# A Fourier convolution before two MoE layers: sums and differences over mirrored positions, one fp32 contraction in the second transform stage

## The chip, the cores and the metric

One core of a Trainium2 chip runs the whole program. The metric is the device time of one execution in microseconds; three runs of the kernel before took 2845.25, 2845.48 and 2846.35 us, median 2845.48. TensorE (PE) multiplies matrices into PSUM, VectorE (DVE) and ScalarE (ACT) read PSUM and SBUF, GpSimd (POOL) works on SBUF, SyncE (SP) issues DMAs.

## What is computed

A long convolution along the sequence, done by Fourier transforms, gated by its own input, and two feed-forward layers behind it:

```python
batch, seq, d_model = 2, 12480, 128
h_filt = (np.maximum(pos_emb @ w1, 0.0) @ w2) * np.exp(-0.01 * pos)[:, None]
u = x * v
y = irfft(rfft(u, 2 * S) * rfft(h_filt, 2 * S)[None], 2 * S)[:, :S]
x = (x * y).reshape(B * S, D)          # 24960 tokens of 128
h = x @ w_in;   x = (h * np.cos(h)) @ w_out            # d_ff 2048
h = x @ w_in2;  x = (h * clip(h + 3, 0, 6) / 6) @ w_out2
```

All inputs are fp32.

## The kernel before

The transform has length N = 111 x 113 (a prime-factor split, `N1` = 111 and `N2` = 113). The sequence sits in a grid of 111 partitions by 113 columns, and two transforms of this length, of the signal and of the signal times the alternating sign `sig`, take the place of one of double length. The 113 columns of a channel stand in mirrored order: 0 to 56, then the mirror of 1 to 56.

First comes the filter stage: 15 chunks of up to four columns for each half (`mlp`, `filt`). PE makes `rp` (plain fp32, one weight tile `w1b`) and then `hps` (`fp32r` matmuls in threes), ACT rounds `rh`, DVE takes the rest `rl`, and DVE multiplies `hps` by the window into three tiles of `h`. The pool `ps_r` holds two `rp` banks. The constants are issued as DMAs from ACT's queue at chunks 5 and 7, the input tiles from SP's.

Then the convolution loop, `NG` = 64 turns, each for two channels of both batches. Software pipelining is written out by hand, and `manual_schedule` keeps each engine's instructions in the order of the code. Turn i does, for PE:

- `s1(i+1, 2)`, `s1(i+1, 0)`, `s1(i+1, 1)`: the first forward stage for the filter and the two batches. Four plain fp32 matmuls each; the data (`h`, `hm`, `u`, 113 columns) is the loaded operand and the constant `f1` (112 columns) is streamed. ACT rounds the result `ap` to `fp32r` (`ah`), DVE subtracts for the rest (`al`).
- between them `s2i(i-2, 0)` and `s2i(i-2, 1)`: the first inverse stage, plain fp32, `bp`; again ACT rounds (`bh`) and DVE takes the rest (`bl`).
- `s2h(i)` and `s2u(i)`: the second forward stage, into `xh` and `xp`. Each of the two outputs (real, imaginary) takes two contractions over 113 rows, and each contraction three `fp32r` matmuls (`cs_h` x `ah`, `cs_h` x `al`, `cs_l` x `ah`): 12 matmuls for `xh` (224 columns) and 12 for `xp` (448).
- `s1i(i-2)`: the last inverse stage, two contractions of three `fp32r` matmuls, `v1` and `v2`.

An fp32 matmul shows as two records in the trace, an `fp32r` one as one. DVE multiplies the spectra (`mk_pq`: `pq` and, in place, `xp`), sums them (`mk_y`), and makes `w` out of `v1` and `v2s`, a copy by ACT (`mk_w`, with a small ACT copy of one column ahead of it). POOL makes `u` = x * v and its product with `sig` (`make_u`), `hm` = h * `sig` (`make_hm`), and the gated output `z` (`fin`), which SP stores. Beside this, `step_decode` unpacks the MoE weights in 16 pieces: four instructions each on DVE (those that fall together make three in one turn and one in another), four on ACT, two on POOL.

PSUM is full: two banks `ps_a` (for `ap` and `xh`), two `ps_x`, two `ps_b`, two `ps_v`. After the loop a tail finishes three channel pairs and hands the first tokens to the MoE stage, which fills the rest of the time.

Of the kernel before, what the change touches and what calls it, by code (L numbers as in the profile page):

```python
# [43 lines left out]
def kernel(  # L44
# [103 lines left out]
    def conv_phase(cctx):  # L148
# [14 lines left out]
        sig = const.tile([NP1, N2], FP32, name="sig")  # L163
        cs_h = const.tile([N2, 3, MP], F32R, name="cs_h")
        cs_l = const.tile([N2, 3, MP], F32R, name="cs_l")
        g_h = const.tile([2 * K1, 2, NP1], F32R, name="g_h")
        g_l = const.tile([2 * K1, 2, NP1], F32R, name="g_l")
# [679 lines left out]
```

## Time and profile before

| | us |
|---|---|
| median of 3 runs | 2845.48 |
| the profiled execution | 2846.66 |
| its span | 2844.9 |
| PE busy | 2812.9 |
| DVE busy | 2419.4 |
| POOL busy | 2406.7 |
| ACT busy | 2156.5 |

The span is what the profiler saw between the first and the last instruction; 1.8 us of the execution lie outside. Busy shares are means over three stages (filter, convolution, MoE) that differ, so the sections below read single stages. In the rows, a time is in microseconds from the start of the span; "x8" is a number of records put together; in square brackets stands how long the engine was idle and what ended that.

### The profile page before, as it was taken

The numbers are of one execution on the slowest core, as the hardware profiler recorded it, in microseconds if no ns is written. First come the engines' busy times: TensorE is split into PE (matmuls) and PEld (weight loads), VectorE is DVE, ScalarE is ACT, GpSimd is POOL, SyncE is SP. The second block draws the span as 40 slices with busy tenths as digits, with TensorE's granted clock in tenths as the row PEclk, the third lists the DMA queues.
The fourth block names the chain that finished last, engine by engine and source line by source line (L and its number), as shares of the span: only waits on it lengthen the run. The fifth ranks groups of instructions, "written<-read, shape, count | busy, mean of one in ns | idle before, by whom it ended". The sixth has DMA issues, their size and how long they took to land.

```text
span 2844.9 us, 41000 instructions
## 1 busy us (share of the span) xinstructions
PE 2812.9 (99%) x14089; PEld 2342.2 (82%) x14089; DVE 2419.4 (85%) x3271; ACT 2156.5 (76%) x3084; POOL 2406.7 (85%) x1390
## 2 busy tenths in 40 slices
PE   8999999998999999999999999999999999999999
PEld 6999999987888888888888888888888888888888
DVE  6888888887888888888888888888888888888887
ACT  2555545448888888888888888888888888888885
POOL 2788888767888888888888888888888889888887
PEclk9999999998999999999999999999999999999999
DMA  3233323210000000000000000000000000000000
GB/s 111 67 92 84 90 78 84 70 50 24 8 16 16 8 16 8 15 16 8 16 8 16 8 16 16 8 15 8 16 16 8 16 8 16 14 10 16 8 8 11
DMA packets 88273, 79.39 MB, mean 28 GB/s; under 512 B 57129, under 2 KB 78852, under 8 KB 88068
## 3 DMA queue, kind: packets, MB, share of 16 engines
q1 hardware_dynamic: 87182, 76.18, 9.7%
q8 instruction: 113, 1.85, 0.3%
q14 instruction: 92, 0.75, 0.1%
q10 hardware_dynamic: 886, 0.60, 0.1%
HBM read 51.00 MB, written 25.74 MB: 27 GB/s over the span
## 4 chain that ended last, share of the span: by engine, by line
PE 91%; DVE 3%; DMA 2%; POOL 1%; ACT 1%; issue 1%; SPq 0%; POOLq 0%; DVEq 0%; ACTq 0%
PE acc L680 38%; PE hb L614 19%; PE ha L614 19%; PE ap L229 4%; PE xp L340 4%; PE xh L340 3%; PE bp L395 2%; PE v L418 2%; DMA scr<-z 1%; DVE y L371 1%; DVE pq L361 1%; DVE xp L361 1%; POOL z L459 1%; POOL z L468 0%; PE hps L287 0%
## 5 line engine op out<-in xcount | busy, mean ns | idle before, releaser
L670 POOL TENSOR_TENSOR lo<-g,hi 128x1024 fp32r<-128x1024 f32 (+1 forms) x390 | 937.4, 2404 | 240.2 <-PE ha L614 162.4
L645 POOL TENSOR_TENSOR lo<-g,hi 128x1024 fp32r<-128x1024 f32 (+1 forms) x392 | 942.4, 2404 | 10.2 <-ACT hi L642 7.6
L635 DVE TENSOR_TENSOR g<-ha,r 128x512 f32<-128x512 f32 (+1 forms) x768 | 499.8, 691 | 289.1 <-ACT r L634 289.1
L624 ACT ACTIVATE k<-ha,biasq 128x512 int32<-128x512 f32 (+1 forms) x768 | 510.3, 689 | 310.2 <-PE ha L614 305.9
L614 PE MATMUL ha<-xh,wi 128*128 128x512 f32 (+1 forms) x1536 | 548.3, 398 | 10.8 <-ACT xh L591 7.7
L614 PE MATMUL hb<-x2h,vi 128*128 128x512 f32 (+1 forms) x1564 | 554.0, 395 | 0.3 <-DVE g L635 0.3
L634 ACT ACTIVATE r<-r,biaspi 128x512 f32<-128x512 f32 (+1 forms) x776 | 520.5, 721 | 0.2
L625 DVE SCALAR_TENSOR_TENSOR r<-k,ha 128x512 f32<-128x512 int32 (+1 forms) x768 | 490.0, 679 | 3.7 <-ACT k L624 3.2
L653 DVE SCALAR_TENSOR_TENSOR g<-q,hb 128x1024 f32<-128x1024 f32 (+1 forms) x391 | 473.2, 1210 | 9.0 <-ACT q L652 9.0
L667 DVE SCALAR_TENSOR_TENSOR hi<-q,hb 128x1024 fp32r<-128x1024 f32 (+1 forms) x390 | 470.1, 1205 | 0.0
L652 ACT ACTIVATE q<-hb,bias 128x1024 f32<-128x1024 f32 (+1 forms) x391 | 435.2, 1113 | 21.4 <-PE hb L614 18.3
L680 PE MATMUL acc<-hi,wo 128*128 128x512 f32 (+1 forms) x1568 | 430.7, 396 | 0.0
L680 PE MATMUL acc<-hi,vo 128*128 128x512 f32 (+1 forms) x1568 | 427.3, 394 | 0.0
L642 ACT CAST hi<-g 128x1024 fp32r<-128x1024 f32 (+1 forms) x388 | 403.6, 1040 | 0.0
L614 PEld LDWEIGHTS ha<-xh,wi 128*128 128x128 f32 x1536 | 289.3, 188 | 80.0 <-issue 11.9
L614 PEld LDWEIGHTS hb<-x2h,vi 128*128 128x128 f32 x1564 | 295.6, 189 | 70.3 <-ACT k L624 0.7
L680 PEld LDWEIGHTS acc<-hi,wo 128*128 128x128 f32 x1568 | 296.8, 189 | 68.4
L680 PEld LDWEIGHTS acc<-hi,vo 128*128 128x128 f32 x1568 | 294.5, 188 | 65.2
L614 PE MATMUL hb<-x2l,vi 128*128 128x512 f32 (+1 forms) x782 | 307.5, 393 | 0.0
L614 PE MATMUL ha<-xl,wi 128*128 128x512 f32 (+1 forms) x768 | 302.4, 394 | 0.0
L680 PE MATMUL acc<-lo,wo 128*128 128x512 f32 (+1 forms) x784 | 246.7, 396 | 0.0
L680 PE MATMUL acc<-lo,vo 128*128 128x512 f32 (+1 forms) x784 | 243.9, 392 | 0.0
(150 smaller groups left out, 3882.2 us busy)
## 6 DMA issues: line engine op xcount, KB each, us to landing
x<-in_x_dram SPq DMA_DIRECT2D x64, 197.8 KB
v<-in_v_dram SPq DMA_DIRECT2D x64, 197.8 KB
scr<-z SPq DMA_DIRECT2D x128, 98.9 KB
out_dram<-o SPq DMA_DIRECT2D x47, 256.0 KB
xf<-scr SPq DMA_DIRECT2D x17, 256.0 KB
wst<-in_wi_dram SPq DMA_DIRECT2D x8, 512.0 KB
wst<-in_wo_dram SPq DMA_DIRECT2D x8, 512.0 KB
pt<-in_post_dram SPq DMA_DIRECT2D x14, 224.0 KB
```

What stands on the lines that cost most here:

```text
L614: nc.tensor.matmul(out=hs[c][:, 0, :n], lhsT=w["i", e][:, sl], rhs=r[:, :n], start=(k == 0), stop=(k == 2))
L624: nc.scalar.activation(out=k[:, c, :n], in_=h, func=ACTF.Identity, bias=biasq, scale=1.0 / TWO_PI)
L625: nc.vector.scalar_tensor_tensor(out=un.r[:, c, :n], in0=k[:, c, :n], scalar=-TWO_PI, in1=h, op0=ALU.mult, op1=ALU.add)
L634: nc.scalar.activation(out=rc, in_=rc, func=ACTF.Sin, bias=biaspi, scale=1.0)
L635: nc.vector.tensor_tensor(out=un.g[:, c, :n], in0=h, in1=rc, op=ALU.mult)
L642: nc.scalar.copy(un.hi[:, :, :n], un.g[:, :, :n])
L645: nc.gpsimd.tensor_tensor(out=un.lo[:, :, :n], in0=un.g[:, :, :n], in1=un.hi[:, :, :n], op=ALU.subtract)
L652: nc.scalar.activation(out=un.r[:, c, :n], in_=h, func=ACTF.Relu, bias=bias3, scale=1.0)
L653: nc.vector.scalar_tensor_tensor(out=un.g[:, c, :n], in0=un.r[:, c, :n], scalar=6.0, in1=h, op0=ALU.min, op1=ALU.mult)
L667: nc.vector.scalar_tensor_tensor(out=un.hi[:, c, :n], in0=un.r[:, c, :n], scalar=6.0, in1=h, op0=ALU.min, op1=ALU.mult)
L670: nc.gpsimd.tensor_tensor(out=un.lo[:, :, :n], in0=un.g[:, :, :n], in1=un.hi[:, :, :n], op=ALU.subtract)
L680: nc.tensor.matmul(out=acc[e][:, :n], lhsT=w["o", e][:, sl], rhs=r[:, c, :n], start=(u == 0 and c == 0 and k == 0), stop=(u == KFF // 2 - ...
```

## The change

The first forward stage no longer carries the 113 columns but their sums and differences with the mirrored position. The column order becomes 1 to 56, 0, and then the mirror of 1 to 56, padded to `MP` = 114, so that both halves have 57. The sum of the halves stands in rows 0 to 56 of the first stage's result, the difference in rows 64 to 120 (`OD` = 64, `KE` = 121), and the rows between are zero. Cosines apply to sums, sines to differences, so real and imaginary part of the second stage are one contraction over 121 rows each, in plain fp32, and the splitting into `fp32r` parts falls away, in the inverse stages too.

```diff
+        def make_q(i):
+            if i >= NG:
+                return
+            q = q_t[i] = p_u.tile([N1, B, 2, CH, M2], FP32, tag="q", name="q")
+            nc.gpsimd.tensor_tensor(
+                out=q[:, :, 0], in0=x_t[i][:N1, :, :, M2:], in1=v_t[i][:N1, :, :, M2:], op=ALU.mult
+            )
+            for b in range(B):
+                nc.gpsimd.tensor_tensor(out=q[:, b, 1], in0=q[:, b, 0], in1=sg(1, CH), op=ALU.mult)
+
         def make_u(i):
             if i >= NG:
                 return
-            u = u_t[i] = p_u.tile([N1, B, 2, CH, N2], FP32, tag="u", name="u")
-            v = v_t.pop(i)
-            nc.gpsimd.tensor_tensor(out=u[:, :, 0], in0=x_t[i][:N1], in1=v[:N1], op=ALU.mult)
+            q, v, u = q_t.pop(i), v_t.pop(i), uf[i % 2]
+            p = ps_p.tile([N1, B, 2, CH, M2], FP32, tag="p", name="p")
+            nc.vector.tensor_tensor(
+                out=p[:, :, 0], in0=x_t[i][:N1, :, :, :M2], in1=v[:N1, :, :, :M2], op=ALU.mult
+            )
             for b in range(B):
-                nc.gpsimd.tensor_tensor(
-                    out=u[:, b, 1], in0=u[:, b, 0],
-                    in1=sig[:N1].unsqueeze(1).to_broadcast([N1, CH, N2]), op=ALU.mult,
-                )
-
-        def make_hm(i):
+                nc.vector.tensor_tensor(out=p[:, b, 1], in0=p[:, b, 0], in1=sg(0, CH), op=ALU.mult)
+            pf, qf, f = (t.rearrange("p b s c n -> p (b s c) n") for t in (p, q, u))
+            for o, op in ((0, ALU.add), (OD, ALU.subtract)):
+                nc.vector.tensor_tensor(out=f[:, :, o:o + M2], in0=pf, in1=qf, op=op)
...
+        def make_hf(i):
             if i >= NG:
                 return
-            hm = hm_t[i] = p_u.tile([N1, CH, N2], FP32, tag="hm", name="hm")
+            hm = p_u.tile([N1, CH, MP], FP32, tag="hm", name="hm")
+            h = h_of(i * CH, CH)
             nc.gpsimd.tensor_tensor(
-                out=hm, in0=h_of(i * CH, CH),
-                in1=sig[:N1].unsqueeze(1).to_broadcast([N1, CH, N2]), op=ALU.mult,
+                out=hm, in0=h, in1=sig[:N1].unsqueeze(1).to_broadcast([N1, CH, MP]), op=ALU.mult
             )
-
-        ps_a = cctx.enter_context(tc.tile_pool(name="ps_a", bufs=2, space=PSUM))
-
-        def s1(i, g):
+            for s_, t in enumerate((h, hm)):
+                for o, op in ((0, ALU.add), (OD, ALU.subtract)):
+                    nc.gpsimd.tensor_tensor(
+                        out=hf[i % 2][:, s_, :, o:o + M2], in0=t[:, :, :M2], in1=t[:, :, M2:], op=op
+                    )
+
+        def s1(i, g, pool=None):
             if i >= NG:
...
-            if True:
-                ap = ps_a.tile([N2, 4, 2 * K1], FP32, tag="a", name="ap")
-                for q in range(4):
-                    s, c = divmod(q, CH)
-                    if g < 2:
-                        st = u_t[i][:, g, s, c, :]
-                    elif s == 0:
-                        st = h_of(i * CH + c)[:, 0, :]
-                    else:
-                        st = hm_t[i][:, c, :]
-                    nc.tensor.matmul(out=ap[:, q, :], lhsT=st, rhs=f1)
-                nc.scalar.copy(ah[:, 4 * g:4 * g + 4, :], ap)
-                nc.vector.tensor_tensor(
-                    out=al[:, 4 * g:4 * g + 4, :], in0=ap, in1=ah[:, 4 * g:4 * g + 4, :], op=ALU.subtract
-                )
+                a_t[i] = p_2.tile([KE, 2, 12, K1], FP32, tag="at", name="at")
+            at = a_t[i]
+            ap = (pool or ps_a).tile([KE, 4, 2, K1], FP32, tag="a", name="ap")
+            for q in range(4):
+                s, c = divmod(q, CH)
+                st = (uf[i % 2][:, g, s, c] if g < 2 else hf[i % 2][:, s, c])[:, :KE]
+                nc.tensor.matmul(out=ap[:, q].rearrange("p z k -> p (z k)"), lhsT=st, rhs=f1)
+            src = ap.rearrange("p q z k -> p z q k")
+            nc.scalar.copy(at[:OD, :, 4 * g:4 * g + 4, :], src[:OD])
+            nc.scalar.copy(at[OD:, ::-1, 4 * g:4 * g + 4, :], src[OD:])
...
-            ps_r = hctx.enter_context(tc.tile_pool(name="ps_r", bufs=2, space=PSUM))
+            ps_r = hctx.enter_context(tc.tile_pool(name="ps_r", bufs=1, space=PSUM))
...
                 hps = ps_h.tile([N1, CB, 2, D], FP32, tag="hps", name="hps")
+                raw = hr.tile([N1, CB, 2, D - HS[2]], FP32, tag="raw", name="raw")
...
+                nc.scalar.copy(raw[:, :n], hps[:, :n, :, HS[2]:])
                 for e in range(2):
-                    m = min(n, (M2, N2 - M2)[e] - c0)
-                    if m <= 0:
-                        continue
+                    m = n
                     j0 = e * M2 + c0
-                    for q, t in enumerate(h_p):
+                    nc.gpsimd.tensor_tensor(
+                        out=h_p[2][:, :, j0:j0 + m].rearrange("p d c -> p c d"),
+                        in0=raw[:, :m, e],
+                        in1=win[:, j0:j0 + m].unsqueeze(2).to_broadcast([N1, m, D - HS[2]]),
+                        op=ALU.mult,
+                    )
+                    for q, t in enumerate(h_p[:2]):
...
                 filt(k)
+                if k == len(chunks) - 3:
+                    make_u(0)
                 if k >= len(chunks) - 2:
                     s1(0, k - len(chunks) + 2)
+                if k == 3:
+                    nc.sync.dma_start(out=sig, in_=c_sig)
+                    load(0)
+                    nc.sync.dma_start(out=f1, in_=c_f1)
+                    nc.sync.dma_start(out=cs, in_=c_cs)
                 if k == 5:
-                    nc.scalar.dma_start(out=sig, in_=c_sig)
-                    load(0)
-                    nc.scalar.dma_start(out=f1, in_=c_f1)
-                    nc.scalar.dma_start(out=cst, in_=c_cs)
-                    make_u(0)
+                    make_q(0)
+                    load(1)
+                    nc.sync.dma_start(out=f2, in_=c_f2)
+                    nc.sync.dma_start(out=gm, in_=c_g)
                 if k == 7:
-                    load(1)
-                    nc.scalar.dma_start(out=f2, in_=c_f2)
-                    nc.scalar.dma_start(out=gst, in_=c_g)
-                    make_u(1)
+                    make_q(1)
                 if k == 9:
                     load(2)
-                    for hi, lo, st in ((cs_h, cs_l, cst), (g_h, g_l, gst)):
-                        nc.scalar.copy(hi, st)
-                        nc.gpsimd.tensor_tensor(out=lo, in0=st, in1=hi, op=ALU.subtract)
...
-        ps_b = cctx.enter_context(tc.tile_pool(name="ps_b", bufs=1, space=PSUM))
+        ps_c = cctx.enter_context(tc.tile_pool(name="ps_c", bufs=1, space=PSUM))
         ps_v = cctx.enter_context(tc.tile_pool(name="ps_v", bufs=1, space=PSUM))
+
         def s2_mm(o, q0, q1, a):
-            ah, al = a
-            hr, hm_, lr, lm = (t[:, q0:q1, z * K1:(z + 1) * K1] for t in (ah, al) for z in range(2))
-            for z, terms in ((0, ((0, hr, lr), (1, hm_, lm))), (1, ((0, hm_, lm), (2, hr, lr)))):
-                k = 0
-                for m, h_, l_ in terms:
-                    for w_, r_ in ((cs_h, h_), (cs_h, l_), (cs_l, h_)):
-                        nc.tensor.matmul(out=o[z], lhsT=w_[:, m, :N2], rhs=r_, start=(k == 0), stop=(k == 5))
-                        k += 1
+            for z in range(2):
+                nc.tensor.matmul(out=o[z], lhsT=cs[:, z, :], rhs=a[:, z, q0:q1, :])
...
         def s2h(i):
-            ap = ps_a.tile([N2, 2, 4, K1], FP32, tag="a", name="xh")
+            ap = ps_c.tile([N2, 2, 4, K1], FP32, tag="a", name="xh")
             s2_mm((ap[:, 0], ap[:, 1]), 8, 12, a_t[i])
...
+        def s2i(i, g, pool=None):
+            if not 0 <= i < NG:
+                return
+            if i not in b_t:
+                b_t[i] = p_2.tile([2 * K1, 8, MP], FP32, tag="b", name="b")
+            src = (pool or ps_a).tile([2 * K1, 4, MP], FP32, tag="a", name="bp")
+            for q in range(4):
+                nc.tensor.matmul(out=src[:, q, :], lhsT=y_t[i][:, 4 * g + q, :], rhs=f2)
+            nc.scalar.copy(b_t[i][:, 4 * g:4 * g + 4, :], src)
...
-            for z, o, sl in ((1, v2, slice(MC, MP)), (0, v1, slice(0, MC))):
-                for k, (w_, r_) in enumerate(((g_h, bh), (g_h, bl), (g_l, bh))):
-                    nc.tensor.matmul(out=o, lhsT=w_[:, z, :], rhs=r_[:, :, sl], start=(k == 0), stop=(k == 2))
-            v1_t[i], v2_t[i] = v1, v2
...
+                    v = ps_v.tile([NP1, 2, 512], FP32, tag="v", name="v")
+                v2_t[i] = p_1.tile([NP1, 8, M2], FP32, tag="v2s", name="v2s", bufs=2)
+                v1_t[i] = [v[:, z, :8 * M2].rearrange("p (a b) -> p a b", b=M2) for z in range(2)]
+            v, b = v1_t[i], b_t[i]
+            r = slice(0, 8) if bs is None else slice(4 * bs, 4 * bs + 4)
+            for z in (1, 0):
+                nc.tensor.matmul(out=v[z][:, r], lhsT=gm[:, z, :], rhs=b[:, r, z * M2:(z + 1) * M2])
+            nc.scalar.copy(v2_t[i][:, r], v[1][:, r])
...
                 r = slice(0, 8) if isinstance(b, slice) else slice(4 * b, 4 * b + 4)
-                nc.scalar.copy(o[:, :, 0:1], v1[:, r, 0:1])
-                eng.tensor_tensor(out=o[:, :, 1:M2], in0=v1[:, r, 1:M2], in1=v2s[:, r], op=ALU.add)
-                eng.tensor_tensor(out=o[:, :, M2:], in0=v1[:, r, 1:M2], in1=v2s[:, r], op=ALU.subtract)
+                for h, op in ((0, ALU.add), (M2, ALU.subtract)):
+                    nc.vector.tensor_tensor(out=o[:, :, h:h + M2], in0=v1[:, r], in1=v2s[:, r], op=op)
...
-        make_hm(0)
+        make_hf(0)
         s1(0, 2)
-        make_hm(1)
+        make_u(1)
+        make_hf(1)
         for i in range(NG):
             load(i + 3)
             store(i - 4)
             s1(i + 1, 2)
             s2i(i - 2, 0)
-            s1(i + 1, 0)
+            s1(i + 1, 0, ps_c)
             s2i(i - 2, 1)
             s1(i + 1, 1)
-            make_u(i + 2)
-            make_hm(i + 2)
+            make_q(i + 2)
+            make_hf(i + 2)
             s2h(i)
             if i >= 3:
                 mk_w(i - 3)
+            make_u(i + 2)
+            if i >= 3:
                 fin(i - 3)
```

Not shown: the column order and the constants follow the new order, `h`, `x`, `v`, `w` and `z` have 114 columns instead of 113, and the tail behind the loop is written with the new functions. `mk_y`, `mk_pq`, the decoder and the MoE stages are the same.

**DVE, one turn of the loop that carries three decoding instructions.** Before (`al`, `bl`: the rests for the `fp32r` parts; `w`: the output sums; `wmh`, `wex`: weight decoding; `pq`, `xp`, `y`: the spectra):

```order
L401 TENSOR_TENSOR bl<-bp_3567,bh 112x456
L231 TENSOR_TENSOR al<-ap,ah 113x448
L401 TENSOR_TENSOR bl<-bp_3581,bh 112x456
L231 TENSOR_TENSOR al<-ap,ah 113x448
L449 TENSOR_TENSOR w<-v_3534,v2s 112x8x56
L450 TENSOR_TENSOR w<-v_3534,v2s 112x8x56
L121 SCALAR_TENSOR_TENSOR wmh<-wst,wmh 128x512
L110 TENSOR_SCALAR wex<-wst 128x512
L111 TENSOR_SCALAR wmh<-wst 128x512
L361 TENSOR_TENSOR pq<-xp,hs 113x896
L361 TENSOR_TENSOR xp<-xp,hs 113x2x448
L371 TENSOR_TENSOR y<-pq,xp 113x8x56 x2
```

and after (`p`: first half of the signal in PSUM; `uf`: sums and differences, the loaded operand of the first stage):

```order
L379 TENSOR_TENSOR xp<-xp,hs 113x2x448
L389 TENSOR_TENSOR y<-pq,xp 113x8x56 x2
L436 TENSOR_TENSOR w<-v,v2s 112x8x57 x2
L215 TENSOR_TENSOR p<-x,v 111x2x114
L219 TENSOR_TENSOR p<-p,sig 111x114 x2
L222 TENSOR_TENSOR uf_85<-p,q 111x8x57 x2
L110 TENSOR_SCALAR wex<-wst 128x512
L111 TENSOR_SCALAR wmh<-wst 128x512
L121 SCALAR_TENSOR_TENSOR wmh<-wst,wmh 128x512
L379 TENSOR_TENSOR pq<-xp,hs 113x896
L379 TENSOR_TENSOR xp<-xp,hs 113x2x448
L389 TENSOR_TENSOR y<-pq,xp 113x8x56 x2
```

The five subtractions `al` and `bl` are gone; `w` follows on `y` at once, and the five instructions of `make_u`, which POOL did before, stand between `w` and the decoding, ahead of `pq`.

**POOL, one turn.** Before (`z`: gated output; `wmh`: decoding; `u`, `hm`: operands of the first stage):

```order
L125 TENSOR_TENSOR wmh<-wex,wmh 128x512
L193 TENSOR_TENSOR u<-x,v 111x2x226
L195 TENSOR_TENSOR u<-u,sig 111x226 x2
L204 TENSOR_TENSOR hm<-h_77,sig 111x226
L459 TENSOR_TENSOR z<-w,sig 112x226 x2
L467 TENSOR_TENSOR z<-z,w 112x452
L468 TENSOR_TENSOR z<-z,x 112x452
```

and after (`q`: second half of the signal; `hf`: sums and differences of the filter):

```order
L128 TENSOR_TENSOR vi<-wmh,vi 128x512
L204 TENSOR_TENSOR q<-x,v 111x2x114
L208 TENSOR_TENSOR q<-q,sig 111x114 x2
L229 TENSOR_TENSOR hm<-h_78,sig 111x228
L234 TENSOR_TENSOR hf_86<-h_78 111x2x57 x2
L234 TENSOR_TENSOR hf_86<-hm 111x2x57 x2
L445 TENSOR_TENSOR z<-w,sig 112x228 x2
L453 TENSOR_TENSOR z<-z,w 112x456
L454 TENSOR_TENSOR z<-z,x 112x456
```

The products `u` are replaced by `q`, half as long, and four instructions on 2 x 57 elements for `hf` follow `hm`; `z` is behind them as before.

**PE, one turn.** Before, from the first stage on (`ap`, with `bp` of the first inverse stage between) to the first three of the 24 matmuls of the second stage (`xh` of the filter, then `xp` of the signal, 12 each, and six `v` of the last inverse stage):

```order
L229 MATMUL ap<-f_79,h_76 113x112 x2
L229 MATMUL ap<-f_79,hm 113x112 x2
L395 MATMUL bp_2155<-f_80,y 112x114 x4
L229 MATMUL ap<-f_79,u 113x112 x4
L395 MATMUL bp_2169<-f_80,y 112x114 x4
L229 MATMUL ap<-f_79,u 113x112 x4
L340 MATMUL xh<-ah,cs_h 113x224
L340 MATMUL xh<-al,cs_h 113x224
L340 MATMUL xh<-ah,cs_l 113x224
```

and after, a whole turn:

```order
L249 MATMUL ap<-f_79,hf_87 121x112 x4
L403 MATMUL bp<-f_80,y 112x114 x4
L249 MATMUL ap<-f_79,uf_85 121x112 x4
L403 MATMUL bp<-f_80,y 112x114 x4
L249 MATMUL ap<-f_79,uf_85 121x112 x4
L359 MATMUL xh<-at,cs 113x224 x2
L359 MATMUL xp<-at,cs 113x448 x2
L417 MATMUL v<-b,gm 112x456 x2
```

Twelve `xh`, twelve `xp` and six `v` become two each, and `ap` loads 121 columns instead of 113; the order of the groups is the same.

## Rows read from the trace of the kernel before

**Rows 1.** Windows, whole loop: start:end, length, busy time (instructions) by engine, clock, DMA.

```profile
53.60:625.38 571.78, 567.45 (x4359) 524.64 (x4359) 478.79 (x746) 275.57 (x558) 442.08 (x514) 1.00 0.29 77
```

**Rows 2.** Chain of waits: start, length, what; first and last `xp`.

```profile
53.60 2.48 PE xp L340 x12
...
625.38 2.46 PE xp L340 x12
```

**Rows 3.** Chain of waits, a plain turn and one with decoding.

```profile
219.07 2.46 PE xp L340 x12
221.53 1.29 PE v L418 x6
222.82 0.79 PE ap L229 x8
223.61 0.79 PE bp L395 x8
...
226.77 1.26 PE xh L340 x12
228.03 2.46 PE xp L340 x12
...
234.98 1.04 PE ap L229 x8
...
237.56 2.46 PE xp L340 x12
```

**Rows 4.** Timeline of DVE: start, length, instruction, idle before; the same two turns.

```profile
229.84 0.42 DVE L110 TENSOR_SCALAR wex<-wst 128x512 int32<-128x512 int32 x1
...
231.11 1.09 DVE L361 TENSOR_TENSOR pq<-xp,hs 113x896 f32<-113x896 f32 x1
...
240.05 1.09 DVE L361 TENSOR_TENSOR pq<-xp,hs 113x896 f32<-113x896 f32 x1 [0.66 <-PE xp L340]
241.06 1.09 DVE L361 TENSOR_TENSOR xp<-xp,hs 113x896 f32<-113x896 f32 x1
242.18 1.15 DVE L371 TENSOR_TENSOR y<-pq,xp 113x448 f32<-113x448 f32 x2
243.25 0.62 DVE L231 TENSOR_TENSOR al<-ap,ah 113x448 fp32r<-113x448 f32 x1
```

**Rows 5.** Chain of waits, filter stage.

```profile
9.37 0.75 PE rp L272 x2
10.12 1.42 PE hps L287 x12
...
47.11 0.67 POOL hm L204
```

**Rows 6.** Groups by line and form, whole trace: count, busy, mean ns, idle before.

```profile
L680 PEld LDWEIGHTS acc<-hi,wo 128*128 128x128 f32 x1568 | 296.8, 189 | 68.4
...
L229 PEld LDWEIGHTS ap<-f,u 111*113 111x113 f32 x1024 | 112.3, 180 | 7.6 <-DVE al L231 7.6
...
L230 ACT CAST ah<-ap 113x448 fp32r<-113x448 f32 x192 | 102.2, 532 | 102.4 <-PE ap L229 102.4
```

**Rows 7.** Timeline of POOL, a turn with decoding and the next.

```profile
230.06 2.12 POOL L459 TENSOR_TENSOR z<-w,sig 112x226 f32<-112x226 f32 x2 [0.93 <-issue]
...
234.50 1.14 POOL L193 TENSOR_TENSOR u<-x,v 111x452 f32<-111x452 f32 x1
235.72 1.30 POOL L195 TENSOR_TENSOR u<-u,sig 111x226 f32<-111x226 f32 x2
236.98 0.67 POOL L204 TENSOR_TENSOR hm<-h,sig 111x226 f32<-111x226 f32 x1
239.52 1.13 POOL L459 TENSOR_TENSOR z<-w,sig 112x226 f32<-112x226 f32 x2 [1.87 <-ACT wex L113]
```

**Rows 8.** Timeline, filter stage, DVE and ACT's queue.

```profile
11.76 2.00 DVE L294 TENSOR_TENSOR h<-hps,win 111x144 f32<-111x144 f32 x6
...
24.11 7.05 ACTq L319 DMA_DIRECT2D gst<-in_g_dram  x1
```

More of the change, by code (lines that the diff above doesn't have):

```diff
@@ L28 @@
 M2 = 57
-MP = 114
-MC = 58
-MS = 56
+MP = 2 * M2
+OD = 64
+KE = OD + M2
 CH = 2
@@ L162, in conv_phase @@
         f2 = const.tile([N2, MP], FP32, name="f2")
[L163 to L167, printed above, removed]
+        sig = const.tile([NP1, MP], FP32, name="sig")
+        cs = const.tile([KE, 2, N2], FP32, name="cs")
+        gm = const.tile([2 * K1, 2, NP1], FP32, name="gm")
+        uf = [const.tile([N1, B, 2, CH, 128], FP32, name=f"uf{k}") for k in range(2)]
+        hf = [const.tile([N1, 2, CH, 128], FP32, name=f"hf{k}") for k in range(2)]
+        for k in range(2):
+            nc.gpsimd.memset(uf[k], 0.0)
+            nc.gpsimd.memset(hf[k], 0.0)
         p_x = cctx.enter_context(tc.tile_pool(name="p_x", bufs=7))
@@ L176, in step_decode @@
                 next(lanes[k], None)
-        x_t, v_t, u_t, hm_t, a_t, hs_t, xp_t, pq_t, y_t, b_t, v1_t, v2_t, w_t, wa_t, z_t = ({} for _ in range(15))
+        x_t, v_t, a_t, hs_t, xp_t, pq_t, y_t, b_t, v1_t, v2_t, w_t, wa_t, z_t = ({} for _ in range(13))
         def load(i):
@@ L381, in s2i_mm, with s1i @@
+        def s1i(i, bs=None, last=False):
+            if i not in v1_t:
                 if last:
-                    tiles = [p_2.tile([N2, 12, 2 * K1], F32R, tag=tag, name=f"{tag}z") for tag in ("ah", "al")]
-                    b_t[i] = [
-                        t.rearrange("p a b -> p (a b)")[:2 * K1, :8 * MP].rearrange("p (a b) -> p a b", b=MP) for t in tiles
-                    ]
-                else:
-                    bh = p_1.tile([2 * K1, 8, MP], F32R, tag="bh", name="bh")
-                    bl = p_1.tile([2 * K1, 8, MP], F32R, tag="bl", name="bl")
-                    b_t[i] = (bh, bl)
@@ L390, in s2i_mm @@
-            if last:
-                src = ps_a.tile([2 * K1, 4, MP], FP32, tag="a", name="bpz")
-            else:
-                src = ps_b.tile([2 * K1, 4, MP], FP32, tag=f"bp{g}", name=f"bp{g}")
-            for q in range(4):
-                nc.tensor.matmul(out=src[:, q, :], lhsT=y[:, 4 * g + q, :], rhs=f2)
-            return src
-        def s2i_ev(i, g, src):
-            bh, bl = b_t[i]
-            nc.scalar.copy(bh[:, 4 * g:4 * g + 4, :], src)
-            nc.vector.tensor_tensor(out=bl[:, 4 * g:4 * g + 4, :], in0=src, in1=bh[:, 4 * g:4 * g + 4, :], op=ALU.subtract)
@@ L508, in pass_on @@
                 d = i * CH + c
[L509 to L522 removed]
+                nc.sync.dma_start(out=x0[d:d + 1, :].rearrange("c (n m) -> c n m", m=N2), in_=z_t[i][:XW // N2, 0, c, :N2])
+        s2i(n - 2, 0)
+        s2i(n - 2, 1)
+        mk_w(n - 3)
+        s2i(n - 1, 0, ps_c)
+        s2i(n - 1, 1)
+        s1i(n - 2)
+        s1i(n - 1, 0, True)
+        s1i(n - 1, 1)
         mk_w(n - 2, (0,))
[L524 removed]
         store(n - 4)
```

102 lines of the change are left out of this document (31 added, 71 removed).

## The prediction

> **What bounds the kernel now.** I read the busy time of the convolution loop first, then the chain of waits through two of its turns, then the timelines of DVE and POOL, and last the head. The loop runs from the first `xp` group at 53.60 to the last at 625.38 us, 63 turns [rows 2]; in these 571.78 us PE is busy 567.45, DVE 478.79, POOL 442.08 and ACT 275.57 us [rows 1]. So one turn takes 9.08 us on average, with 9.01 of PE, 7.60 of DVE, 7.02 of POOL and 4.37 of ACT.
>
> The chain shows the same thing finer: in a plain turn it never leaves PE. From 219.07 to 228.03 it is `xp` 2.46, `v` 1.29, five groups `ap`/`bp` of 0.79 each (222.82 to 226.77) and `xh` 1.26, together 8.96 us [rows 3]. Every turn in which DVE carries three weight-decoding instructions is longer: the next `xp` starts at 237.56, 9.53 after the last, because a group of `ap` starts late at 234.98 [rows 3]. 16 of the 63 turns are of that kind, at about 9.54, and nearly all others take 8.95; 16 x 9.54 + 47 x 8.95 = 573 is the loop to within its first and last turns. The reason stands in the DVE timeline: `pq` comes 1.27 us after the first decoding instruction (229.84 to 231.11), while in a plain turn DVE stands idle for only 0.66 before `pq` [rows 4]. The difference, about 0.6 us, pushes the `al` subtractions behind `y` back, and the PSUM bank of a later `ap` group is not free in time.
>
> What counts is therefore the PE work of a turn, with the DVE work of a decoding turn close behind.
>
> **PE, the term that decides.** The second forward stage goes from 24 `fp32r` matmuls (12 of 224 columns, 12 of 448) to 4 plain fp32 ones (two of 224, two of 448). The price of a plain fp32 matmul is in the head: `rp`, 448 columns, 0.75 us [rows 5]. So `xp` costs 2 x 0.75 = 1.50 instead of 2.46, and `xh` 2 x 0.375 = 0.75 instead of 1.26. The last inverse stage goes the other way: six `fp32r` matmuls become two fp32 ones of 456 columns, 2 x 0.75 x 456/448 = 1.53 instead of 1.29. Its columns come in short pieces; `v` has 2736 columns in 1.29 us against 5376 of `xp` in 2.46, 3% more per column, so up to 1.57.
>
> `bp` stays at 2 x 0.79. `ap` keeps its 112 streamed columns, but its loaded operand grows from 113 to 121 columns (sums in rows 0 to 56, differences from 64). Two bounds: if streaming sets its 0.79, nothing changes, 3 x 0.79 = 2.37; if the weight load does, it grows by 121/113 to 2.54. `ap` loads 113 and streams 112, `bp` loads 112 and streams 114, and both step at 0.79 [rows 3], so the row itself doesn't decide. That loads do take longer with columns shows in the MoE stage: 189 ns for 128 columns against 180 for 113 [rows 6]. I take the upper end, 2.54. By TensorE: Matmul & The Clock Gate, section LDWEIGHTS, of the Trainium skill, a load takes its column count over 1.2 GHz whatever the rows; that would be 8/1.2 = 6.7 ns for each of 24 loads, 0.16 us a turn, an estimate from that page. The rows give 9 ns for 15 columns, about 0.12 a turn.
>
> Sum of a turn: 1.50 + 0.75 + 1.57 + 1.58 + 2.54 = **7.94 us**, from below 7.73. If PE stays the bound, 63 turns take 500.2 us instead of 571.8: **71.6 us** gained (up to 84.8 at 7.73).
>
> **DVE, the cover that must hold.** It loses three `al` and two `bl` (0.535 each, from the two `y` between 242.18 and 243.25 [rows 4]), 2.68 us. From 896 elements in 1.01 and 448 in 0.535 I get 1.06 ns an element plus 0.06; a dependent successor adds 0.11 (`xp` to `y`, 1.12 instead of 1.01). It gains `p` = x*v, 228 elements, 0.30 + 0.11; two times 114, 0.36 + 0.11; sum and difference, 2 x 0.545. That is 1.97. A turn is then `w` 1.09, the five above 1.97, `pq`, `xp` and `y` 3.20: 6.26, and 7.53 with the decoding instructions. Both are under 7.94, so the 0.58 that each of the 16 turns loses now should vanish (it is already in the 9.08). `make_u` stands between `w` and the decoding, so `pq` queues behind it; the margin in a decoding turn is 0.41 us.
>
> `w` is no longer behind ACT's small copy of one column, which DVE waited for. In its place `make_u` waits for POOL's `q`, but POOL makes `q` at the start of a turn and DVE reads it after `w`.
>
> **POOL.** `u` (452 elements, 1.22 to its dependent successor) and two of 226 (1.26 together) and `hm` (0.63) [rows 7] become `q` of 228 (0.63), two of 114, `hm` of 228 (0.63) and four of 114. No row shows 114 elements on POOL. In proportion to 226 in 0.63 and 452 in 1.22 they cost 0.32, at worst as much as 226, 0.63. I take 0.32, since 226 is already near half of 452: 0.63 + 0.63 + 6 x 0.32 = 3.18 against 3.11 now. So POOL stays near 7.1 us a turn.
>
> **ACT.** Evacuating `ap` takes two copies (64 and 57 partitions, 448 elements each) instead of one; a copy is 0.53 [rows 6]. With 6 for `ap`, two of `b`, `hs` and `v2s`, ten in all: 5.3 us a turn, which leaves 2.6 for the decoding work of some turns. The chain that matters is the PSUM bank: `ap` group 0.85, drain and two copies, about 2.1 us from the start to a free bank, and the third group after it starts 2.48 after. That just fits, and is the tightest place on ACT.
>
> **Head and tail.** Now a chunk of the filter takes PE 0.75 + 1.42 = 2.17, and DVE 2.00 for six `h` and some 0.4 to 0.5 for `rl` (448 elements), so DVE sets the pace; the ACT queue then stands 7.05 us at the issue of `gst`, and `hm` starts at 47.11 [rows 5, 8]. After, DVE has four `h`, 1.33, and `rl`, under 1.9; ACT has one more copy, POOL two products of 224 elements (0.63 each), and constants are issued by SP, where nothing computes. With one `rp` bank instead of two, `rp` waits for `rl` of the chunk before, so a chunk costs about 2.25 and the start comes some 1.3 later: 9.37 + 1.3 = 10.7 for the `rp` that is at 9.37 now, 13 chunks, 29.3, and 1.4 for `make_u(0)` in DVE's queue: 41.4. Before the first `xp` there are then `hf(0)`, `hf(1)` (about 1.9 each on POOL, where `hm` takes 0.67 now), three `ap` groups and `xh`, 3.8 + 3 x 0.85 + 0.75 = 7.1, less some 0.4 where they overlap: 48.1 instead of 53.6. Gain 5.5, taken as **5**; none if POOL's transposed writes set the pace, 8 at best. The tail behind the last `xp` is a chain through the same DVE, POOL and DMA steps: 0, give or take 2. The MoE stages after it are the same instructions.
>
> **Sum.** 71.6 + 5 = 76.6 us off the profiled span of 2844.9: 2768.3. The profiled execution took 2846.66, 1.2 above the median of 2845.48, so against the median it is 2768.9: **2769**.
>
> **Rivals.** (1) DVE and POOL get in each other's way. At 230.06 two `z` products took 2.12 us on POOL, against 1.13 in a plain turn for the same two, while DVE ran its decoding instructions, `wmh<-wst,wmh` with two SBUF operands among them, and these were not stretched [rows 4, 7]. `p<-x,v` is a new DVE instruction with two SBUF operands, and it starts at the moment when `w` releases POOL's `z`, in every turn. If POOL loses 1 us a turn and DVE is held for one POOL product (0.6), a decoding turn has no margin and a plain one little: 8.3 to 8.6 us a turn, 63 x 8.45 = 532, gain 40 + 5, **2801**. For it: the 2.12. Against it: plain turns have 1.7 us of DVE margin (7.94 - 6.26) and 0.8 of POOL. SBUF — State Buffer, section Who interferes with whom, of the Trainium skill has this as a rule: a DVE instruction with two SBUF inputs and a POOL instruction that reads SBUF exclude each other, and the later one waits for the whole of the first. The trace agrees in the one direction that it shows.
>
> (2) Slower: POOL becomes the bound. If an instruction of 114 elements costs what one of 226 does, six of them cost 6 x 0.31 = 1.9 more and POOL is at 9.0 us a turn; with 0.5 lost to DVE it is 9.5. From 9.16 on, the head's gain is eaten too. 63 x 9.5 = 598.5: 27 lost, 5 gained, **2867**. Against it: the near proportion of 226 to 452.
>
> (3) It does not do what it says: `ap` groups wait for ACT's second copy, or `xp` for late operands, each turn by about 1.1 us, and the loop stays at 9.0: gain 5 at most, **2843**. Against it: ACT's 5.3 of 7.94 us.
>
> **How the numbers follow.** PE-bound loop at 7.73 to 8.1 us: 0.74 (2755 to 2782). Rival 1: 0.17. Rival 3: 0.03, of which 0.02 within 0.2%. Rival 2: 0.04. The rest, 0.02, is a faster head than bounded. The range takes in the lower bound and most of rival 1: 2754 to 2799. Differences of under 0.2%, 5.7 us, can't be told from no change here. Faster 0.94, same 0.02, slower 0.04.
>
> **What would show it.** A plain turn of 7.9 us from `xp` to `xp` with the chain on PE alone; `xp` 1.50, `xh` 0.75, `v` 1.53 to 1.57, `ap` 0.85 (0.79 if the load doesn't count); decoding turns as long as plain ones; `hf` products of 114 elements near 0.3 us; first `xp` near 48 us. Idle time of PE that ends on ACT `at`, POOL `hf` or DVE `uf` would show rivals 3, 2 and 1.

## The result, and the profile after

| | before | after |
|---|---|---|
| device time, median | 2845.76 us (2845.25 to 2846.35) | 2804.90 us (2804.27 to 2805.42) |
| profiled execution, span | 2844.9 us | 2802.5 us |
| first `xp` group | 53.60 us | 57.27 us |
| first to last `xp` group, 63 turns | 571.78 us | 530.03 us |
| last `xp` group to the end | 2219.5 us | 2215.2 us |

The changed kernel takes 0.9855 of the time (95% interval 0.9842 to 0.9869): 41 us less. The forecast was 77 us less, 2769, with a range that ended at 2799. Of the 42.4 us between the two spans, the loop gave 41.75 and the tail 4.3, and the head took 3.7 back. The forecast had 71.6 from the loop, 5 from the head and 0 from the tail.

The page of after, share of the chain that ended last by engine:

```profile
PE 84%; POOL 13%; DVE 1%; ACT 1%; issue 1%; DMA 0%; POOLq 0%; SPq 0%; ACTq 0%; DVEq 0%
```

In before POOL has 1% there. The busy time of the engines between the first and the last `xp` group (us, then the number of instructions in brackets), to be laid beside [rows 1]:

```profile
core 0: us, PE busy (x) PEld busy (x) DVE busy (x) ACT busy (x) POOL busy (x), PEclk, DMA share, GB/s
57.27:587.30 530.03, 510.64 (x3230) 392.30 (x3229) 465.49 (x742) 367.24 (x685) 495.65 (x757) 0.99 0.31 83
```

PE has 19 us of idle time where it had 4, and POOL is busy 93% of the time where it had 77%. The loop has two stretches. After the weight decoding has ended, the chain of waits is a plain turn on PE alone (start, duration, what; it answers to [rows 3]):

```profile
542.51 1.50 PE xp L359 x4
544.01 1.56 PE v L417 x4
545.57 0.84 PE ap L249 x8
546.41 0.79 PE bp L403 x8
...
549.67 0.76 PE xh L359 x4
550.43 1.50 PE xp L359 x4
```

From `xp` to `xp` it is 7.92 us. While weights are decoded it is another chain. From 222.06 to 248.47 us, three turns, no piece is PE's: all are POOL's, but for pieces of issue time of 0.22 us at most; the middle turn:

```profile
228.15 1.16 POOL z L454
229.31 1.23 POOL wmh L125
230.54 0.78 POOL q L204
...
231.40 0.77 POOL q L208 x2
232.17 0.59 POOL hm L229
...
233.06 1.85 POOL hf L234 x3
234.92 1.17 POOL z L445 x2
...
238.55 1.23 POOL wo L128
239.78 0.78 POOL q L204
```

POOL does not stand still for 26.4 us, and three turns of PE take 23.8; from 94 to 500 us no gap on POOL is longer than 0.13 us. Of PE's idle time from 120 to 480 us the view of waits has one line, with the sum, the count and the longest:

```profile
PE ap L249 <- POOL hf L234: 16.0, 13, 1.5
```

The next two views show what makes POOL late there. DVE (start, duration, line, out<-in):

```profile
233.29 0.68 DVE L117 SCALAR_TENSOR_TENSOR wex<-wst,wex 128x512 int32<-128x512 int32 x1
...
238.17 1.87 DVE L215 TENSOR_TENSOR p<-x,v 111x228 f32<-111x228 f32 x1
...
242.54 0.68 DVE L121 SCALAR_TENSOR_TENSOR wmh<-wst,wmh 128x512 f32<-128x512 uint32 x1
243.14 0.42 DVE L110 TENSOR_SCALAR wex<-wst 128x512 int32<-128x512 int32 x1
243.48 0.42 DVE L111 TENSOR_SCALAR wmh<-wst 128x512 int32<-128x512 int32 x1
...
248.09 0.65 DVE L215 TENSOR_TENSOR p<-x,v 111x228 f32<-111x228 f32 x1
```

POOL in the same turns, and, last, in a turn without decoding:

```profile
232.72 1.50 POOL L234 TENSOR_TENSOR hf<-h 111x114 f32<-111x114 f32 x2
...
238.51 1.27 POOL L128 TENSOR_TENSOR wo<-wmh,wo 128x512 fp32r<-128x512 f32 x1
...
241.96 2.18 POOL L234 TENSOR_TENSOR hf<-h 111x114 f32<-111x114 f32 x2
```

```profile
524.14 0.68 POOL L204 TENSOR_TENSOR q<-x,v 111x228 f32<-111x228 f32 x1
...
526.25 0.74 POOL L234 TENSOR_TENSOR hf<-h 111x114 f32<-111x114 f32 x2
...
531.27 0.68 POOL L204 TENSOR_TENSOR q<-x,v 111x228 f32<-111x228 f32 x1
```

The first `hf` pair (sum and difference of `h`) takes 0.74 us in a plain turn. It takes 1.50 when `wex` (L117) runs on DVE, and 2.18 when `wmh`, `wex` and `wmh` (L121, L110, L111) do; in both cases the pair ends 0.25 us after DVE's last decoding instruction. So DVE's decoding shuts POOL out, for 0.76 + 1.44 = 2.2 us per weight tile. It works the other way too: `p<-x,v` takes 0.65 where POOL has one instruction left and 1.87 where `z` and then the decode product `wo` (238.51, 1.27) are on POOL; it ends just after both.

### The profile page after: what moved, and what is told of

Same layout as the page of the kernel before. It is cut to its first block, busy times and chain, and to the rows that moved or that the text cites. A ratio compares the mean times of both kernels' runs of the same rounds, so it can differ in the third digit from the quotient of the medians.

```text
span 2802.5 us, 39594 instructions
## 1 busy us (share of the span) xinstructions
PE 2755.2 (98%) x12941; PEld 2204.8 (79%) x12941; DVE 2397.1 (86%) x3246; ACT 2254.3 (80%) x3223; POOL 2476.6 (88%) x1676
## 4 chain that ended last, share of the span: by engine, by line
PE 84%; POOL 13%; DVE 1%; ACT 1%; issue 1%; DMA 0%; POOLq 0%; SPq 0%; ACTq 0%; DVEq 0%
PE acc L664 39%; PE hb L598 20%; PE ha L598 19%; POOL hf L234 3%; PE ap L249 2%; POOL z L445 2%; POOL z L454 2%; POOL z L453 2%; POOL q L208 1%; POOL q L204 1%; PE bp L403 1%; PE xp L359 1%; POOL hm L229 1%; PE v L417 1%; POOL wmh L125 1%
```

## The experiments

All are edits of the changed kernel. The loop is always measured between the first and the last `xp` group; in after it is 530.0 us. e1, e9, e10 and e11 were timed four times (median, lowest and highest are given), the others once.

**e1: the decode products on DVE.** This tests whether POOL is too full (A) or DVE's queue too late (B).

```diff
-        nc.gpsimd.tensor_tensor(out=m, in0=ex.bitcast(FP32), in1=m, op=ALU.mult)
+        nc.vector.tensor_tensor(out=m, in0=ex.bitcast(FP32), in1=m, op=ALU.mult)
...
-        nc.gpsimd.tensor_tensor(out=wl, in0=m, in1=wh, op=ALU.subtract)
+        nc.vector.tensor_tensor(out=wl, in0=m, in1=wh, op=ALU.subtract)
```

> The two decode products per weight tile (128x512, 1.27 us each on POOL, 32 in the loop) run on DVE instead. Theory A (POOL is full while weights are decoded: 7.2 us of its own work a turn, 0.87 of decode products, about 0.75 in which it is held during DVE's decode instructions, together 8.8): about 0.87 a turn goes, some of it comes back since the products now hold POOL from DVE; turns of 7.95 to 8.3 in the decode stretch, loop 503 to 512 us instead of 530, total 2777 to 2788. Theory B (DVE's queue is what is late, through the long x*v product): DVE gets 16 x 1.1 us more, loop 530 to 548, total 2805 to 2823.

Measured: loop 525.8 us, time 2801.4 (2799.95 to 2801.73), 0.984 of before (0.9824 to 0.9856). Neither range holds it: A was too hopeful by 14 us, and B had the wrong sign. DVE's timeline shows why:

```profile
233.53 1.01 DVE L117 SCALAR_TENSOR_TENSOR wex<-wst,wex 128x512 int32<-128x512 int32 x1
234.47 1.64 DVE L128 TENSOR_TENSOR wo<-wmh,wo 128x512 fp32r<-128x512 f32 x1
...
243.46 1.37 DVE L110 TENSOR_SCALAR wex<-wst 128x512 int32<-128x512 int32 x1
244.75 0.90 DVE L111 TENSOR_SCALAR wmh<-wst 128x512 int32<-128x512 int32 x1
```

The `hf` pairs are back at 0.73, POOL stands idle for up to 1.7 us a turn, and DVE's decoding instructions wait for POOL instead: `wex` L110 takes 1.37 where it took 0.42, `wo` 1.64. The chain of the decode stretch is now DVE's, with turns of 8.02, 8.56 and 9.54. What is lost in being shut out moved from one engine to the other.

**e2: the new product with one SBUF operand.** `p<-x,v` is the instruction that the prediction's first rival suspected.

```diff
-            nc.vector.tensor_tensor(
-                out=p[:, :, 0], in0=x_t[i][:N1, :, :, :M2], in1=v[:N1, :, :, :M2], op=ALU.mult
+            nc.scalar.copy(p[:, :, 0], x_t[i][:N1, :, :, :M2])
+            nc.vector.tensor_tensor(
+                out=p[:, :, 0], in0=p[:, :, 0], in1=v[:N1, :, :, :M2], op=ALU.mult
```

> ACT copies the x half into the PSUM tile of p, and DVE's product reads PSUM and v instead of x and v, so that it has one SBUF operand and no longer lasts 1.0 to 1.9 us. Theory A: DVE only waits elsewhere (for POOL's q); loop 524 to 530 us, total 2799 to 2805. Theory B: the 0.65 us a turn by which the product is long now is what is missing; loop 503 to 508 us, total 2778 to 2783.

Measured: loop 526.7, time 2804.0 (the first `xp` comes 2.9 us later), as theory A had it. The product is short now, 0.40 everywhere, and the loop gets 3.3 us shorter, where after loses 36.7 against what PE needs (e6): the product was not the main cause. On POOL the hold went to another instruction, a `z` product that lasts 2.66 us instead of 1.16 while L110, L111 and L121 run on DVE (273.14 to 274.49):

```profile
272.86 2.66 POOL L454 TENSOR_TENSOR z<-z,w 112x456 f32<-112x456 f32 x1
```

**e3 and e4: a little more work on POOL, and on DVE.**

```diff
+            nc.gpsimd.tensor_tensor(
+                out=hf[i % 2][:, 1, :, OD:OD + M2], in0=hm[:, :, :M2], in1=hm[:, :, M2:], op=ALU.subtract
+            )
```

> One hf difference (114 elements, 0.36 us on POOL) is done twice in each turn. Theory A: each of some 44 turns in the decode stretch gets 0.36 to 0.4 longer, the last 11 turns stay at 7.93; loop 546 to 549 us, total 2821 to 2824. Theory B: POOL waits for nobody's bound, loop 530 to 533.

```diff
+            nc.vector.tensor_tensor(out=p[:, 1, 1], in0=p[:, 1, 0], in1=sg(0, CH), op=ALU.mult)
```

> One 114-element product of make_u (0.28 us on DVE, PSUM source) is done twice in each turn. Theory A: nothing, loop 529 to 532 us, total 2804 to 2807. Theory B: 0.28 in each of 44 turns, loop 542 us, total 2817.

Measured: e3 loop 552.1, time 2828.4; e4 loop 530.4, time 2806.1. One instruction of 0.39 us on POOL costs 22 us, somewhat more than the 16 to 19 expected, all of it in the decode stretch (the nine turns before the last stay at 7.93). One of 0.28 us on DVE costs nothing. POOL is the bound there, DVE is not.

**e5: without DVE's decoding instructions.** ACT reads the raw words, so that the weights hold other values.

```diff
-        nc.vector.tensor_scalar(ex, hi, 20, 0x7FF, op0=ALU.logical_shift_right, op1=ALU.bitwise_and)
-        nc.vector.tensor_scalar(mh, hi, 0xFFFFF, None, op0=ALU.bitwise_and)
...
-        nc.vector.scalar_tensor_tensor(
-            out=ex, in0=hi, scalar=-0x80000000, in1=ex, op0=ALU.bitwise_and, op1=ALU.bitwise_or
...
-        nc.vector.scalar_tensor_tensor(
-            out=m, in0=lo.bitcast(UINT32), scalar=2.0 ** -52, in1=m, op0=ALU.mult, op1=ALU.add
...
```

> DVE's four decoding instructions are left out (ACT reads the raw words, so the weights hold other values); POOL keeps the two products of each weight tile. It splits POOL's extra load: 0.87 us a turn of products, about 0.75 of being held while DVE decodes. Theory A (both count, POOL is full): 7.2 + 0.87 = 8.07 in the decode stretch, loop 505 to 511 us, total 2780 to 2786. If the holds are absorbed anyway and only the products count: loop about 528 us. If only the holds count: 500 us.

```profile
57.30:552.55 495.25, 494.26 (x3229) 387.36 (x3229) 415.71 (x678) 367.72 (x685) 461.08 (x757) 1.00 0.33 89
```

Measured: loop 495.3, time 2769.7, below all three expected values. 34.8 us of the loop go with four DVE instructions, though e4 showed that DVE has time to spare: they cost through POOL. 16 tiles times the 2.2 us read from the `hf` pairs are 35.2. The products alone cost little, and there theory A was too high: POOL's own turn is 7.13 us back to back (524.14 to 531.27 in after), and two products of 1.23 in three turns make 7.95, next to PE's 7.93.

**e6: the decoding behind the loop.**

```diff
-            step_decode()
             s2u(i)
...
+        for _ in range(60):
+            step_decode()
```

> The weight decoding runs after the convolution loop instead of in it. Theory A, and any theory that blames the decoding: all turns 7.93, loop 499 to 502 us. If the long turns came from the new instructions by themselves, the loop stays above 515. The total gets longer, since the decoding now stands by itself: about 7.4 us for each of 8 tasks of a lane, 60 us, less the 30 of the loop: 2825 to 2845.

```profile
58.11:551.43 493.32, 492.42 (x3230) 387.47 (x3229) 395.08 (x678) 326.10 (x621) 420.60 (x724) 1.00 0.26 74
```

Loop 493.3 us, below the 499 to 502 expected: all turns are 7.92 to 8.03 but the first two (5.95, 6.37) and the last (5.39), which lack some groups. This is what PE alone needs. It is busy 492.42 us here and 510.64 in after, so half of what after loses lies in PE's busy time: an `ap` group that starts on the first `hf` pair and waits inside for the second takes 1.37 instead of 1.00 (at 234.28 and 244.20 us), and three turns run in part at the lower clock. The time is 2849.4, also outside its range: after the last `xp`, 81 us more pass.

**e12: without the two decoding instructions that have one SBUF operand** (again the weights hold other values). The first two deleted statements of e5, L110 and L111, go; L117 and L121 stay.

> Of DVE's four decoding instructions the two with one SBUF operand (shift and mask, 0.34 us each back to back) are left out, the two with two SBUF operands stay; ACT reads the raw words, so the weights hold other values. It tells which kind shuts POOL out. If both kinds do: 16 x 0.68 = 11 us off the loop, 517 to 521 us, total 2792 to 2796, and the hf pair that took 2.18 us takes about 1.5. If only the instructions with two SBUF operands do: loop 527 to 530, total 2802 to 2805.

Measured: loop 519.9, time 2795.5, and the long `hf` pair takes 1.51:

```profile
237.98 1.51 POOL L232 TENSOR_TENSOR hf<-h 111x114 f32<-111x114 f32 x2
```

Ten of the 35 us belong to these two. So both kinds shut POOL out, not only those with two SBUF operands.

**e7: the head.** `rp` has two banks again, and the first `ap` groups come behind the last chunk.

```diff
-                rp = ps_r.tile([128, CB, NP1], FP32, tag="rp", name="rp")
+                rp = (ps_a if k % 2 else ps_r).tile([128, CB, NP1], FP32, tag="a" if k % 2 else "rp", name="rp")
...
-                if k >= len(chunks) - 2:
-                    s1(0, k - len(chunks) + 2)
+                if k == len(chunks) - 1:
+                    s1(0, 0)
+                    s1(0, 1)
```

> Head: rp of odd chunks takes a bank of ps_a, so that there are two again, and the ap groups of the first turn come behind the last chunk. If the single bank sets the pace (2.42 us a chunk in after: rp 1.02, rh 0.55, rl 0.63 round the one bank): chunks of 2.17 to 2.25 by PE, and the last chunk is not behind two at copies on ACT any more: first xp at 50 to 53 us instead of 57.3, total 2799 to 2801. If DVE's h behind ACT's raw or POOL's transposed h set the pace: chunks stay at 2.35 to 2.42, first xp 54.5 to 57.

Measured: first `xp` at 49.9 us instead of 57.3, loop 529.7, time 2796.5, a little better than the first of the two expectations. In the chain of after the next `rp` waits for `rl` to clear the one bank, and `rl` stands on DVE behind four `h`, which come after ACT's `raw`; two chunks take 4.81 us. At the end the `raw` copy of the last chunk stands behind two `at` copies on ACT (this answers to [rows 5]):

```profile
13.77 1.02 PE rp L289 x2
14.79 1.45 PE hps L305 x12
...
16.26 0.54 ACT raw L306
...
16.83 1.25 DVE h L317 x4
18.07 0.46 DVE rl L293
...
18.58 1.02 PE rp L289 x2
...
46.13 0.53 ACT at L251
46.66 0.54 ACT at L252
...
47.22 0.26 ACT raw L306
...
47.54 0.54 POOL h L310 x2
48.08 0.72 POOL hm L229
```

The chain of e7 is PE alone, 2.19 us a chunk, to 34.98 us:

```profile
13.04 0.76 PE rp L289 x2
13.79 1.44 PE hps L305 x12
```

**e8, e9, e10, e11: less for POOL to do.** e8 makes one instruction of each of three pairs (one for each batch row); `sgb` is `sig` spread over both batch rows, where `sg` had one:

```diff
-            for b in range(B):
-                nc.gpsimd.tensor_tensor(out=q[:, b, 1], in0=q[:, b, 0], in1=sg(1, CH), op=ALU.mult)
+            nc.gpsimd.tensor_tensor(out=q[:, :, 1], in0=q[:, :, 0], in1=sgb(1), op=ALU.mult)
...
-                nc.vector.tensor_tensor(out=p[:, b, 1], in0=p[:, b, 0], in1=sg(0, CH), op=ALU.mult)
+            nc.vector.tensor_tensor(out=p[:, :, 1], in0=p[:, :, 0], in1=sgb(0), op=ALU.mult)
...
+                eng.tensor_tensor(
+                    out=z, in0=wa_t[i][:, :, 1],
+                    in1=sig.unsqueeze(1).unsqueeze(1).to_broadcast([NP1, B, CH, MP]), op=ALU.mult
...
```

> Three pairs of products, one for each batch row, become one instruction each: q*sig on POOL (2 x 114 to 228 elements), z on POOL (2 x 228 to 456), p*sig on DVE. Theory A: POOL saves 0.15 to 0.23 us a turn, and the turns of the decode stretch get shorter by this on average; loop 520 to 523 us, total 2795 to 2798. If POOL were not full: loop 528 to 530.

> The head of e7 and the merged products of e8 together. They act on different stretches, so the gains should add: first xp at 49.9, loop 517 us, total 2784 (2783 to 2786).

e10 is e9 with the first of e1's two lines. e11 is e9 with the second half's x*v on DVE, a turn ahead:

```diff
+        def start_q(i):
...
+            nc.vector.tensor_tensor(
+                out=q[:, :, 0], in0=x_t[i][:N1, :, :, M2:], in1=v_t[i][:N1, :, :, M2:], op=ALU.mult
...
             make_u(i + 2)
+            start_q(i + 3)
```

> e9, and the first decode product (L125, 16 in the loop) on DVE, in the turn that has no other decoding instruction on DVE. Theory of exclusion (a turn of the decode stretch is POOL's own work, plus its products, plus the time of the DVE instructions that shut POOL out): per three turns POOL loses 1.24 and gains 0.6 of being held, so 15 x 0.65 = 10 us off the loop: 506 to 509, total 2773 to 2777. If DVE is as tight as in e1: loop 515 to 520, total 2782 to 2787.

> e9, and the x*v product of the second half (228 elements, 0.65 to 0.82 us on POOL in every turn) on DVE, one turn ahead. Theory of exclusion: POOL gets rid of 0.7 a turn and is held for 0.3, so 45 turns get 0.35 to 0.4 shorter: loop 500 to 503 us, total 2767 to 2771. If DVE, which now has one more instruction that waits for POOL to let go, becomes the bound: loop 515 to 525, total 2782 to 2792.

| | loop, us | time, us | ratio to before |
|---|---|---|---|
| e8 | 517.3 | 2792.0 | timed once |
| e9 | 516.8 | 2783.9 (2783.58 to 2784.09) | 0.9781 (0.9766 to 0.9795) |
| e10 | 501.5 | 2768.6 (2768.00 to 2768.66) | 0.9727 (0.9710 to 0.9743) |
| e11 | 493.3 | 2761.2 (2759.98 to 2761.29) | 0.9700 (0.9686 to 0.9715) |

e9 came as expected. e8, e10 and e11 gained more than the sums had it, by 3, 5 and 7 us beyond the range. A reason that fits, though no run tried it by itself: a POOL that is not behind is also held less where it matters. In e10 and e11 the `hf` pairs take 0.74 to 0.89, and in e10 it is DVE's L110 that takes up to 1.37. e11 is as fast in the loop as e6, which decodes nothing there:

```profile
50.93:544.27 493.34, 492.75 (x3230) 387.60 (x3229) 465.08 (x741) 367.03 (x684) 433.75 (x572) 1.00 0.34 89
```

```profile
247.11 2.47 POOL L466 TENSOR_TENSOR z<-z,x 112x456 f32<-112x456 f32 x1
```

Its POOL is still held, here for 1.3 us in a `z`, with the four decoding instructions of DVE in place, but with 434 us of work in 493 it catches up. e11 beats both kernels: 85 us under before, 44 under after.

## Why the prediction was wrong, point by point

- **What bounds before, and PE's new turn: right.** The plain turn was forecast at 7.94 and takes 7.92: `xp` 1.50, `xh` 0.76 (0.75), `v` 1.56 (1.57), `bp` 0.79, `ap` 0.84 (0.85 by the upper bound, growing with the loaded columns). 63 turns were put at 500.2; PE needs 493.3 (e6), since three turns at the ends are short. (The long turns of before, 9.46 to 9.55, are 15 and not 16; the sum hardly moves by it.)
- **The step that failed: "POOL stays near 7.1 us a turn".** First, the products were spread over all turns (32 x 1.23 us in 63 turns are 0.62), while they lie in two of three turns of a stretch of some 45. Second, `q`, the pair behind it and the four `hf` instructions were put at 2.55 and take 2.92 in a plain turn from start to start, and POOL's own turn is 7.13, where the forecast's 7.1 less 0.62 left 6.5; that base was low because it is a mean over 63 turns of which only 60 make `u` and `z`. Third, the time in which POOL is shut out has no term of its own. The mean of before carries 1.3 us of it per weight tile (its first two `z` products take 1.46 and 2.12 in turns with decoding, 221.04 and 230.06 us, against 1.13), 0.3 a turn; after has 2.2 per tile, all in the decode stretch. With 7.13, 0.82 and about 0.74 for the holds, and 0.15 for `q` behind `p`, a turn of the decode stretch is 8.8: the three turns of 26.4 us. Over the loop that is 36.7 us more than PE needs, and e5 gives 34.8 of them back.
- **Rival 1 had the size, not the culprit.** 8.45 us a turn, loop 532, time 2801 against 8.41, 530.0 and 2804.9. That the sizes agree is in part luck: the rival spread the loss over all turns, and it falls in the decode stretch alone, at 8.8 a turn, while the others take 7.92. It suspected `p<-x,v`; e2 takes that away and gains 3.3 us. The instructions that shut POOL out are the four decoding ones, which before has as well, unchanged. There POOL still stood idle in such turns (0.93 and 1.87 ahead of `z` in [rows 7]), so the 2.12 us seen in `z` had room to be made up. The change took that idle time away with the shorter turn. The prediction saw the 2.12, and argued it off with the margins of plain turns (0.8 on POOL), which the product in the same turns has already used up. The chance of 0.17 was too small for that, and the range, which ended at 2799, left out the rival's own time.
- The Trainium skill, SBUF — State Buffer, section Who interferes with whom, has the rule that the prediction cited: a DVE instruction with two SBUF inputs and a reading POOL instruction exclude each other. By these runs it holds in both directions (`hf` 0.74 to 1.50, `p` 0.40 to 1.87). The same section has instructions like `tensor_scalar` in a mode that uses both ports do it too. e12 agrees, with 10 us of loop for L110 and L111. That these two run in such a mode is not shown directly; in after they step at 0.34 us, and L121, of as many elements but with two SBUF operands, at 0.60.
- **DVE, the cover that must hold: right where it counted.** e4 shows time to spare, and decoding turns are not longer through DVE. It did wait for POOL's `q`, 34 us over the loop, where the prediction saw no wait; e4 says that this cost nothing. Once DVE is given the products (e1), it becomes the bound.
- **Rivals 2 and 3: did not come as described.** An instruction of 114 elements costs about 0.36 on POOL, not 0.63. No idle time of PE ends on ACT in the decode stretch; all that the view lists ends on POOL's `hf`. In the words of the prediction's last paragraph that is the sign of rival 2, and POOL did become the bound; but the reason that rival 2 gave, costly instructions of 114 elements, is not what made it so.
- **The head: wrong in sign.** First `xp` at 48.1 was forecast, 57.3 came. A chunk takes 2.42 instead of 2.25, 2.2 us in all. Most of the rest up to `hm(0)`, which starts at 48.08 where the sum had 41.4, is the queue at the end: `raw` of the last chunk waits on ACT for the `at` copies, these for PE, and PE for `uf`. The sum looked at each engine's work per chunk and not at the order behind the last one. Behind `hm` another 2.2 us are the clock's (last section). With the bank and the order mended (e7) it is 49.9, near the forecast.
- **The tail** gained 4.3, outside the 0 plus or minus 2. It was not the chain that the prediction meant: the first `ha` matmul of the MoE stage comes 18.0 us after the last `xp` in before and 18.3 in after. The gain lies behind it, some 2 us of it in the first 45 us, where in before the granted clock is 0.83 from 680 to 700 us and in after 1.00 in the stretch that answers to it (642.5 to 662.5), the rest spread over the whole MoE stage. Why has not been tried.

## What to carry to other kernels

When a change shortens the engine that bounds a loop, work out every other engine's turn for the heaviest stretch, not the mean over the loop, and from back-to-back starts, not from durations. Time in which one engine shuts out another is free as long as the victim has idle time, and costs in full once it has not: a stretched instruction in the profile can be a price that is not yet paid. What helps then is to take work off the shut-out engine, as much as the other one has room for: e10 and e11 moved one product of POOL's to DVE and brought the loop from e9's 516.8 to 501.5 and 493.3 us; e1 moved both decode products, DVE became the bound, and the loop went from 530.0 to 525.8 only.

## What was not expected of the hardware

DVE instructions with one SBUF operand (`tensor_scalar`, 512 int32, 0.42 us) also kept POOL waiting: the `hf` pair took 2.18 us with L121, L110 and L111 behind each other, and 1.51 without L110 and L111. A waiting DVE instruction sat out two POOL instructions in a row: `p<-x,v` 1.87.

TensorE's granted clock fell after some of the waits. In after, between 188 and 191.3 us PE waited 1.47 us for `hf`, and then (PEclk is the last number but two):

```profile
188.00:191.30 3.30, 1.91 (x5) 0.53 (x3) 2.66 (x6) 0.54 (x1) 3.30 (x6) 1.00 0.30 81
191.30:196.60 5.30, 5.20 (x32) 5.03 (x33) 5.15 (x9) 2.12 (x5) 5.07 (x9) 0.68 0.00 0
196.60:204.00 7.40, 7.40 (x50) 5.71 (x49) 5.11 (x8) 6.75 (x13) 7.24 (x12) 1.00 0.63 157
```

In the second row the granted clock is 0.68 on average: for a part of it the lower of the two levels, 1.2 GHz, and a `bp` group steps at 1.52 us instead of 0.79. The turn took 11.57 us; three of the 63 are of this kind. Seven other waits of the same length, the one before 244.20 us among them, were not followed by it, and what tells them apart is open. POOL was busy 5.07 of 5.30 us meanwhile, without a gap, so POOL's chain and not the clock set the time there. In the head nothing else covers it. After PE's waits for `uf` and `hf` the three `ap` groups ahead of the first `xh` take 4.75 us, where 3 x 0.84 are 2.5:

```profile
40.00:51.00 11.00, 7.39 (x45) 6.75 (x44) 8.34 (x26) 3.58 (x8) 5.72 (x13) 0.75 0.23 67
51.00:57.40 6.40, 6.20 (x32) 5.72 (x32) 1.77 (x5) 4.08 (x8) 6.24 (x16) 0.63 0.53 163
```

That is 2.2 us of the head. In before the granted clock is 1.00 from 46 to 53.6 us.
